# An attention kernel with a mixture-of-depths layer behind it: scatters that do not wait for each other, a reordered start, denominators in four column tiles, and sections of four attention steps with up to two pieces of the layers

## The chip, the cores and the metric

The kernel runs on one core of a Trainium2 chip. The metric is device time in microseconds (us), the median of the runs shown. A core has five engines with a queue each, which runs in order: TensorE (PE, its weight loads are PEld), VectorE (DVE), ScalarE (ACT), GpSimd (POOL) and SyncE (SP, which here only issues DMAs).

## The reference

```python
q_n, k_n = rmsnorm(q, g_q), rmsnorm(k, g_k)           # (8, 12, 448, 64), fp32
attn = softmax(q_n @ k_n.T / 8); x = attn @ v         # heads side by side: (8, 448, 768)
scores = x @ w_gate                                   # per batch: the 128 tokens of highest score
h = relu(x[top] @ w1); y = h @ w2                     # 768 -> 1024 -> 768
out = x; out[top] = x[top] + sigmoid(scores[top]) * y
```

Eight batches are independent of each other. The layers of a batch need its gate scores, and so all of its attention.

## The kernel before

**Units and groups.** Four heads of a batch are a group (24 groups, three per batch); a group's 448 keys are cut into 7 steps of 64, the *units* (168). `scores` of a unit (L252) fills two banks of `ps_sc` (four banks in all), ACT turns them into `p` by an Exp (L261), `values` (L278) accumulates `p` times v into the group's two banks `av`, and `add_probs` (L291, DVE) adds the `p` of a group's units up. PE works in tiles of 64x32 there, and a group of 32 recorded matmuls is two units.

**End of a group.** ACT and DVE copy `av` out as `xT` (L303, L305); `sum_keys` (L315, called D below) adds `sum` over the partitions into `den_ps`; `invert_sums` (T, L331, L333) transposes it and takes reciprocals; `to_tokens` runs twice (X, L345, L347): PE transposes `xT` into `x_ps` and DVE multiplies it into the tokens `x`. D, T, X and the transposes R of the gate's scores share one bank, the only buffer of `ps_aux`.

**End of a batch.** DVE computes the gate (L368) and spreads it, R and a copy give `score_rows`, DVE ranks the tokens (`count`, L401, four instructions) and prepares the weights (`annotate`, L415 to L426), POOL scatters the chosen rows to DRAM by four indirect DMAs (`select`, L433), SP loads them back (`load_selected`, `xe`), and `mixture` transposes them (E, L463) and runs the two layers as eight *pieces* M (four of L480 and four of L497). The last piece ends in L506 and one indirect DMA into the output.

**Preparation of a group.** SP loads `tok` (queries and keys by token), `qT`, `kT` and `v`; ACT squares `tok` (L167), DVE sums (L173, L174), POOL takes the power -1/2 (`rinv`, L177); for the queries the result goes to DRAM and comes back broadcast (`rows_out`, `rows_in`: `rows`, `bc`), and DVE scales `qT` (L211). For group 0, PE broadcasts instead (L223).

**Order.** The program's order is written out by hand. A *section* is: scores of two units, values of the two units before, then what `at(slot, ...)` has put there, and one piece of `mixture` if it has one left. There are 84 sections. All waits follow from the data and the buffers.

Of the kernel before, what the change touches and what calls it, by code (L numbers as in the profile page):

```python
# [26 lines left out]
def fast(  # L27
# [23 lines left out]

    nc = tc.nc
# [22 lines left out]
    p_pool = ctx.enter_context(tc.tile_pool(name="p", bufs=6))  # L75
# [50 lines left out]
    nc.vector.memset(neg_half, -0.5)  # L126

# [12 lines left out]
    def constants():  # L140


        nc.vector.memset(earlier, -1.2e-38)
# [13 lines left out]
    def load_weights():  # L157
        nc.sync.dma_start(out=wg, in_=_bcast_row(moe_w_gate, CP))
        nc.sync.dma_start(out=w1, in_=moe_w1.rearrange("(c p) f -> p c f", p=128))
        nc.sync.dma_start(out=w2, in_=moe_w2.rearrange("(c p) f -> p c f", p=128))  # L160
# [3 lines left out]
    def squares(n, i):  # L164
        t = toks.pop((n, i))
        sq = norm_pool.tile([128, 2, NI, D], F32, name="sq", bufs=1)
# [144 lines left out]
    def sum_keys(n):  # L311

        ps = ps_aux.tile([128, 512], F32, tag="aux", name="den_ps")
        for hh in range(2):
            nc.tensor.matmul(  # L315
                out=ps[32 * hh : 32 * (hh + 1), 0:S],
                lhsT=pick_pair,
                rhs=sums[n][:, hh],
                start=True,
                stop=True,  # L320
            )
        sums.pop(n)
        den = norm_pool.tile([64, NJ, CP], F32, name="den", bufs=1)
        nc.scalar.copy(out=den, in_=ps[:64, 0:S].rearrange("d (p j) -> d j p", j=NJ))
        dens[n] = den

    def invert_sums(n):
        den = dens.pop(n)
        ps = ps_aux.tile([128, NJ, 64], F32, tag="aux", name="denT_ps")
        for j in range(NJ):  # L330
            nc.tensor.transpose(out=ps[:CP, j, :], in_=den[:, j, :], identity=ident[:64, :64])  # L331
        rden = norm_pool.tile([CP, NJ, 2, 2], F32, name="rden")
        nc.vector.reciprocal(  # L333
            out=rden, in_=ps[:CP].rearrange("p j (h r) -> p j h r", r=32)[:, :, :, 0:2]
        )
        rdens[n] = rden
# [26 lines left out]
    def gate(b, js):  # L363
        if js[0] == 0:
            gates[b] = moe_pool.tile([CP, NJ], F32, name="gate", bufs=2)
        for j in js:
            prod = moe_pool.tile([CP, DM], F32, name="prod")
            nc.vector.scalar_tensor_tensor(  # L368
                out=prod,
                in0=xs[b][:, j, 0:DM],  # L370
                scalar=1.0,
                in1=wg,
                op0=OP.mult,
                op1=OP.mult,
                accum_out=gates[b][:, j : j + 1],
            )

    def spread(b):

        t = moe_pool.tile([CP, NJ, CP], F32, name="spread")  # L380
        nc.vector.tensor_copy(out=t, in_=gates[b][:, :, None].to_broadcast([CP, NJ, CP]))
        rowss[b] = t
# [45 lines left out]
    def select(b):  # L428

        x, rank = xs.pop(b), ranks.pop(b)  # L430
        t = dram_pool.tile([CAP, DX], F32, name="selected")
        for j in range(NJ):
            nc.gpsimd.indirect_dma_start(  # L433
# [6 lines left out]
            )  # L440
        slots_dram[b] = t
# [8 lines left out]
    def mixture(b):  # L450
# [23 lines left out]
        yield  # L474
        hT = moe_pool.tile([128, NFC, 128], F32, name="hT")
        for f0 in range(0, NFC, 2):
            ps = ps_moe.tile([128, 512], F32, tag="moe", name="moe_ps")
            for i in range(2):
                for dc in range(NDC):
# [6 lines left out]
                    )  # L486
            nc.scalar.activation(  # L487
                out=hT[:, f0 : f0 + 2, :n],
                in_=ps[:, :256].rearrange("p (i t) -> p i t", t=128)[:, :, :n],
# [644 lines left out]
```

## Time and profile before

| | us |
|---|---|
| median of 3 runs (lowest, highest) | 658.07 (656.10, 661.79) |
| the profiled execution, its own time | 659.13 |
| its span, first to last instruction | 657.4 |
| PE busy in the span | 546.7 (83%) |
| DVE busy | 359.4 (55%) |
| ACT busy | 276.8 (42%) |
| POOL busy | 186.4 (28%) |
| mean granted TensorE clock | 0.928 of full |

The page divides the span by engine and shows it in 40 slices. Further views show the instructions in order of time with what ended the idle time before them, the waits by who waited for whom, and the busy time in any stretch.

### The profile page before, as it was taken

Reading aid. Unit: us, or ns where it says so; the run is one execution under the profiler, and the core shown is the slowest. Engines: PE = TensorE matmul, PEld = TensorE weight load, DVE = VectorE, ACT = ScalarE, POOL = GpSimd, SP = SyncE. Lnnn points to the kernel's source line nnn. Section 1 sums busy time; section 2 is a strip of 40 time slices with the busy share of each in tenths; the row PEclk is TensorE's granted clock in tenths of the full one; section 3 lists DMA queues with packets and bytes.
Section 4 is the critical chain, followed back from the end, with each engine's and each line's share of the span. In section 5 each row is a group of like instructions: output and inputs, shape, how many; then the busy total and the mean of one; then the engine's idle time right before and its main releaser. Section 6 shows DMA issues by size and latency. Waiting matters only on the chain.

```text
span 657.4 us, 15932 instructions
## 1 busy us (share of the span) xinstructions
PE 546.7 (83%) x6920; PEld 282.4 (43%) x6920; DVE 359.4 (55%) x588; ACT 276.8 (42%) x497; POOL 186.4 (28%) x99
## 2 busy tenths in 40 slices
PE   1638988689997999499996999599998999797185
PEld 1213333246434554156433654256435643284182
DVE  1446879554873568454873558554876476335000
ACT  1335665544544545444543544444544544410000
POOL 2633442511154223412053232512055212100200
PEclk9959998879997999979996999989999999798589
DMA  7975556172706534272806534273706331102200
GB/s 247 397 266 169 171 197 225 41 245 104 251 22 197 195 109 169 67 236 86 253 20 205 187 91 167 68 230 112 252 27 220 113 114 35 40 1 84 72 1 28
DMA packets 46914, 93.99 MB, mean 143 GB/s; under 512 B 11510, under 2 KB 29686, under 8 KB 46836
## 3 DMA queue, kind: packets, MB, share of 16 engines
q1 hardware_dynamic: 43492, 86.58, 39.9%
q0 software_dynamic: 3200, 6.31, 2.9%
q8 instruction: 56, 0.92, 0.6%
q14 instruction: 22, 0.18, 0.1%
q10 hardware_dynamic: 144, 0.00, 0.0%
HBM read 75.39 MB, written 25.36 MB: 153 GB/s over the span
## 4 chain that ended last, share of the span: by engine, by line
PE 53%; issue 21%; DMA 10%; POOL 7%; DVE 5%; ACT 3%; POOLq 0%; SPq 0%; DVEq 0%; ACTq 0%
PE sc L252 16%; PE av L278 13%; PE moe_ps L480 10%; PE moe_ps L497 7%; POOL selected L433 4%; DMA selected<-x,rank 4%; DMA xe<-selected 4%; PE x_ps L345 3%; DMA tok<-in_tok_dram 2%; POOL rinv L177 2%; ACT p L261 2%; DVE ss L173 2%; PE den_ps L315 1%; PE denT_ps L331 1%; DVE sum L291 1%
## 5 line engine op out<-in xcount | busy, mean ns | idle before, releaser
L261 ACT ACTIVATE p<-sc,rinv 128x448 f32<-128x448 f32 x336 | 186.5, 634 | 156.8 <-PE sc L252 141.2
L177 POOL TENSOR_TENSOR rinv<-ss,neg_half 128x14 f32<-128x14 f32 x48 | 136.7, 2848 | 300.6 <-DVE ss L174 280.2
L252 PE MATMUL sc<-qT,kT 64*32 64x448 f32 x2688 | 162.8, 588 | 15.9 <-ACT p L261 11.3
L278 PE MATMUL av<-p,v 64*32 64x448 f32 x2688 | 154.1, 556 | 7.3 <-ACT xT L303 7.3
L291 DVE TENSOR_TENSOR sum<-sum,p 128x896 f32<-128x896 f32 x120 | 129.3, 1077 | 4.7
L480 PEld LDWEIGHTS moe_ps<-xeT,w 128*128 128x128 f32 x768 | 90.5, 196 | 14.9 <-ACT p L261 11.0
L480 PE MATMUL moe_ps<-xeT,w 128*128 128x128 f32 x768 | 95.4, 282 | 1.5 <-ACT hT L487 1.5
L278 PEld LDWEIGHTS av<-p,v 64*32 64x32 f32 x2688 | 54.1, 111 | 90.1 <-issue 73.1
L497 PE MATMUL moe_ps<-w,hT 128*128 128x384 f32 x256 | 91.1, 502 | 1.9 <-DVE xe L506 1.4
L252 PEld LDWEIGHTS sc<-qT,kT 64*32 64x32 f32 x2688 | 46.6, 111 | 83.9 <-issue 60.6
L173 DVE TENSOR_REDUCE ss<-sq 128x14 f32<-128x896 f32 x48 | 51.9, 1080 | 35.1 <-ACT sq L167 35.1
L433 POOL DMA_INDIRECT selected<-x,rank x32 | 38.7, 1210 | 95.0 <-DVE x L426 46.6
L497 PEld LDWEIGHTS moe_ps<-w,hT 128*128 128x128 f32 x256 | 47.1, 193 | 41.7 <-issue 10.3
L347 DVE TENSOR_TENSOR x<-x_ps,rden 112x512 f32<-112x512 f32 x48 | 33.1, 690 | 40.5 <-PE x_ps L345 39.7
L167 ACT ACTIVATE sq<-tok 128x896 f32<-128x896 f32 x48 | 46.2, 962 | 14.8 <-DMA tok<-in_tok_dram 10.2
L487 ACT ACTIVATE hT<-moe_ps 128x256 f32<-128x256 f32 x32 | 12.3, 383 | 88.4 <-PE moe_ps L480 88.4
L345 PE MATMUL x_ps<-ident,xT 128*112 128x128 f32 x192 | 30.5, 281 | 11.9 <-DVE x L347 11.5
L463 PE MATMUL moe_ps<-ident,xe 128*128 128x128 f32 x24 | 6.5, 401 | 40.7 <-DMA xe<-selected 40.7
L506 DVE SCALAR_TENSOR_TENSOR xe<-moe_ps,xe 128x384 f32<-128x384 f32 x16 | 9.9, 618 | 53.2 <-PE moe_ps L497 53.1
L211 DVE SCALAR_TENSOR_TENSOR qT<-qT,gg,bc 128x896 f32<-128x896 f32 x23 | 26.4, 1148 | 17.3 <-DMA bc<-rows 17.3
L345 PEld LDWEIGHTS x_ps<-ident,xT 128*112 128x112 f32 x192 | 20.3, 133 | 32.7 <-DVE x L347 14.0
L305 DVE COPY xT<-av 128x448 f32<-128x448 f32 x24 | 15.0, 624 | 31.0 <-PE av L278 31.0
(54 smaller groups left out, 242.5 us busy)
## 6 DMA issues: line engine op xcount, KB each, us to landing
tok<-in_tok_dram SPq DMA_DIRECT2D x48, 448.0 KB, 6.5
qT<-in_qT_dram SPq DMA_DIRECT2D x24, 448.0 KB, 5.8
kT<-in_kT_dram SPq DMA_DIRECT2D x24, 448.0 KB, 7.6
v<-in_vp_dram SPq DMA_DIRECT2D x24, 448.0 KB, 7.6
out_dram<-x SPq DMA_DIRECT2D x8, 1344.0 KB, 7.3
bc<-rows SPq DMA_DIRECT2D x46, 224.0 KB, 4.0
w<-in_moe_w_dram SPq DMA_DIRECT2D x2, 3072.0 KB, 20.6
xe<-selected SPq DMA_DIRECT2D x8, 385.0 KB, 3.2
```

The source lines that it names most:

```text
L167: nc.scalar.activation(out=sq, in_=t, func=AF.Square, scale=scale)
L173: nc.vector.tensor_reduce(out=ss, in_=sq, axis=AX.X, op=OP.add)
L177: nc.gpsimd.tensor_tensor(out=rinv.rearrange(flat), in0=ss.rearrange(flat), in1=neg_half.to_broadcast([128, 2 * NI]), op=OP.pow,)
L252: nc.tensor.matmul(out=scs[hh][o : o + 32, 0:S], lhsT=kTs[n][r, c, D * i + k0 : D * i + k0 + 32], rhs=qTs[n][r, c, :], start=True, stop=True,)
L261: nc.scalar.activation(out=p[:, hh], in_=scs[hh][:, 0:S], func=AF.Exp, scale=rinvs[n, 1][:, hh, i : i + 1],)
L278: nc.tensor.matmul(out=avs[n][c][o : o + 32, 0:S], lhsT=vs[n][r, hh, i, d0 : d0 + 32], rhs=probs[u][r, hh], start=(i == 0), stop=(i == NI ...
L291: nc.vector.tensor_tensor(out=sums[n], in0=probs[u - 1] if i == 1 else sums[n], in1=probs[u], op=OP.add)
L345: nc.tensor.transpose(out=ps[:CP, j, :], in_=t[:, j, :], identity=ident)
L347: nc.vector.tensor_tensor(out=xs[b][:, :, col : col + 128].rearrange("p j (h d) -> p j h d", d=D), in0=ps[:CP].rearrange("p j (h d) -> p j ...
L433: nc.gpsimd.indirect_dma_start(out=t[:, :], out_offset=bass.IndirectOffsetOnAxis(ap=rank[:, j : j + 1], axis=0), in_=x[:, j, :], in_offset ...
L480: nc.tensor.matmul(out=ps[:, 128 * i : 128 * i + n], lhsT=w1[:, dc, 128 * (f0 + i) : 128 * (f0 + i + 1)], rhs=xeT[:, dc, :n], start=(dc == 0),
L497: nc.tensor.matmul(out=ps[:n, : DM // 2], lhsT=hT[:, fc, :n], rhs=w2[:, fc, cols], start=(fc == 0), stop=(fc == NFC - 1),)
```

## The change

- `select`: the four scatters of a batch are declared independent, so that none waits for the one before to land.
- Start: both `tok` of groups 0 and 1 are squared first, `sq` gets a second buffer, group 1 is prepared ahead of the first scores, and all loads of group 1 stand ahead of the weights, which are loaded in 14 parts at slots 8 to 21. An Exp on one column stands ahead of the first square; `earlier` is set by POOL.
- `values_out`: both copies of `av` on ACT, contiguous (the order of the queries is changed on the host).
- `sum_keys`: four matmuls of 224 columns on four column tiles in place of two of 448; `invert_sums` transposes twice in place of four times.
- `gate`: per group (four instructions of 256 columns each) in place of per batch (four of 768).
- `mixture`: `hT` is filled in fours; the last batch's layers use the banks of `ps_sc`.
- Order: a section is two *halves* (two units each, the values always of the half before, then the half's slots), and then up to two pieces of `mixture`. D, T, X and R are a list of tasks; one of them may go ahead of the first piece and one behind each piece. The section with E holds one piece. There are 42 sections until the last scores, numbered q0 to q41 below.

```diff
-    p_pool = ctx.enter_context(tc.tile_pool(name="p", bufs=6))
+    p_pool = ctx.enter_context(tc.tile_pool(name="p", bufs=7))
...
+    load_tok(0, 1)
     load_q(0)
-    load_tok(0, 1)
     load_k(0)
-    load_v(0)
     load_tok(1, 0)
     load_tok(1, 1)
+    load_v(0)
     load_q(1)
+    load_k(1)
+    load_v(1)
...
+    warm = const.tile([128, 1], F32, name="warm")
+    nc.scalar.activation(out=warm, in_=neg_half, func=AF.Exp)
...
-            src = avs[n][c][:, 0:S].rearrange("d (p j) -> d j p", j=NJ)
-            if c == 0:
-                nc.scalar.copy(out=t, in_=src)
-            else:
-                nc.vector.tensor_copy(out=t, in_=src)
+            nc.scalar.copy(out=t.rearrange("d j p -> d (j p)"), in_=avs[n][c][:, 0:S])
...
+            for odd in range(2):
+                o = 64 * odd + 32 * hh
+                nc.tensor.matmul(
+                    out=ps[o : o + 32, 0 : S // 2],
+                    lhsT=pick_pair,
...
+        for jj in range(NJ // 2):
+            nc.tensor.transpose(out=ps[:CP, jj, :], in_=den[:, jj, :], identity=ident)
...
-    def gate(b, js):
+    def gate(n):
...
-        for j in js:
-            prod = moe_pool.tile([CP, DM], F32, name="prod")
+        cols = slice(GH * D * g, GH * D * (g + 1))
+        for j in range(NJ):
+            prod = moe_pool.tile([CP, GH * D], F32, name="prod")
...
+        writes = []
         for j in range(NJ):
-            nc.gpsimd.indirect_dma_start(
+            w = nc.gpsimd.indirect_dma_start(
...
+            for other in writes:
+                tc.declare_no_dep(w.ins, other.ins, reason="different rows")
+            writes.append(w)
...
+        def bank():
+            if b == B - 1:
+                return ps_sc.tile([128, 512], F32, name="sc")
+            return ps_moe.tile([128, 512], F32, tag="moe", name="moe_ps")
...
+    for part in range(NDC + NFC):
+        at(8 + part, load_w, part)
+    at(9, constants)
...
+    def finish(n, q):
+        b, g = divmod(n, NG)
+        task((q, 1), sum_keys, n)
+        task((q, 2) if HALVES > 1 else (q + 1, 0), invert_sums, n)
+        task((q + 1, 0) if HALVES > 1 else (q + 1, 1), to_tokens, n, 0)
+        task((q + 1, 1) if HALVES > 1 else (q + 2, 0), last_tokens, n)
...
+    def last_tokens(n):
+        to_tokens(n, 1)
+        b, g = divmod(n, NG)
+        q = now[0]
+        at(PER * (q + 1), gate, n)
+        if g < NG - 1:
+            return
+        at(PER * (q + 1), store_x, b)
+        at(PER * (q + 1) + 1, spread, b)
+        task((q + 1, 1), ranks_of, b)
+
+    def ranks_of(b):
+        score_rows(b)
+        s = PER * (now[0] + 1)
+        at(s, count, b, (0, 1))
+        at(s + 1, count, b, (2, 3))
+        at(s + 2, annotate, b)
+        at(s + 2, select, b)
+        at(s + 3, load_selected, b)
+        ready.append((b, (s + 3) // PER + 4 // HALVES - 1))
...
+        for half in range(HALVES):
+            k = 2 * (HALVES * q + half)
+            for u in (k, k + 1):
+                if u < units:
+                    scores(u)
+            run_values(k - 1, q)
+            for slot in (k, k + 1):
+                for fn in todo.pop(slot, ()):
+                    fn()
+        opening(q, 0)
+        for half in range(HALVES):
+            end = next(moe, None)
+            if end is None and ready and q >= ready[0][1]:
+                moe = mixture(ready.pop(0)[0])
+                end = next(moe)
+                done += 1
+            opening(q, half + 1)
+            if end and HALVES > 1:
+                break
+        q += 1
```

PE's order at the turn to the third batch's layers (`moe_ps<-ident,xe` and `xeT_ps` are E, `x_ps` X, `den_ps` D, `denT_ps` T, `row_ps` R; 16 matmuls of `sc` or `av` are two units). Before:

```order
L345 MATMUL x_ps<-ident,xT 112x128 x8
L252 MATMUL sc<-qT,kT 32x448 x16
L278 MATMUL av<-p,v 32x448 x16
L252 MATMUL sc<-qT,kT 32x448 x16
L278 MATMUL av<-p,v 32x448 x16
L315 MATMUL den_ps<-sum,pick_pair 32x448 x2
L463 MATMUL moe_ps<-ident,xe 128x128 x3
L463 MATMUL xeT_ps<-ident,xe 128x128 x3
L331 MATMUL denT_ps<-ident,den 112x64 x4
L252 MATMUL sc<-qT,kT 32x448 x16
L278 MATMUL av<-p,v 32x448 x16
```

Now (from the end of q19 to the end of q21):

```order
L345 MATMUL denT_ps<-ident,den 112x128 x2
L266 MATMUL sc<-qT,kT 32x448 x16
L292 MATMUL av<-p,v 32x448 x24
L266 MATMUL sc<-qT,kT 32x448 x16
L292 MATMUL av<-p,v 32x448 x16
L359 MATMUL x_ps<-ident,xT 112x128 x8
L266 MATMUL sc<-qT,kT 32x448 x16
L292 MATMUL av<-p,v 32x448 x16
L266 MATMUL sc<-qT,kT 32x448 x16
L292 MATMUL av<-p,v 32x448 x16
L488 MATMUL moe_ps<-ident,xe 128x128 x3
L488 MATMUL xeT_ps<-ident,xe 128x128 x3
```

E stands two sections of two units behind X before, and one section of four units behind it now; no piece M lies between them in either.

DVE's order in the section in which that batch is ranked (q20; `cmp` is `count`, `rank` to `x<-token_f` is `annotate`, `ss` the sums of squares, `qT` the scaling). Before, the same batch:

```order
L401 SCALAR_TENSOR_TENSOR cmp,higher<-score_rows,gate,earlier 112x448 x2
L506 SCALAR_TENSOR_TENSOR xe<-moe_ps,xe 128x384
L173 TENSOR_REDUCE ss<-sq 128x14
L174 TENSOR_SCALAR ss<-ss 128x14
L415 CAST rank<-higher 112x4
...
L426 TENSOR_SCALAR x<-token_f 112x4
L333 RECIPROCAL rden<-denT_ps 112x16
L291 TENSOR_TENSOR sum<-sum,p 128x896 x2
L347 TENSOR_TENSOR x<-x_ps,rden 112x4x128 x2
```

Now:

```order
L305 TENSOR_TENSOR sum<-p 128x896
L305 TENSOR_TENSOR sum<-sum,p 128x896
L187 TENSOR_REDUCE ss<-sq 128x14
L421 SCALAR_TENSOR_TENSOR cmp,higher<-score_rows,gate,earlier 112x448 x2
L225 SCALAR_TENSOR_TENSOR qT<-qT,gg,bc 128x896
L421 SCALAR_TENSOR_TENSOR cmp,higher<-score_rows,gate,earlier 112x448 x2
L305 TENSOR_TENSOR sum<-sum,p 128x896 x2
L187 TENSOR_REDUCE ss<-sq 128x14
L188 TENSOR_SCALAR ss<-ss 128x14
L435 CAST rank<-higher 112x4
...
L446 TENSOR_SCALAR x<-token_f 112x4
L361 TENSOR_TENSOR x<-x_ps,rden 112x4x128 x2
```

All that DVE does for a section of four units stands now ahead of the first product `x<-x_ps`, for which the second X of PE waits, since both use the one bank. Before, `annotate` came a section after `count`, and L506 of the layers stood between them.

SP's order at the start. Before:

```order
L91 DMA tok<-in_tok_dram 128x896
L91 DMA qT<-in_qT_dram 128x2x448
L91 DMA tok<-in_tok_dram 128x896
L91 DMA kT<-in_kT_dram 128x2x448
L91 DMA v<-in_vp_dram 128x896
L91 DMA tok<-in_tok_dram 128x896 x2
L91 DMA qT<-in_qT_dram 128x2x448
L158 DMA wg<-in_moe_w_gate_dram 112x768
L159 DMA w_143<-in_moe_w_dram 128x6x1024
L160 DMA w_144<-in_moe_w_dram 128x8x768
L91 DMA kT<-in_kT_dram 128x2x448
L91 DMA v<-in_vp_dram 128x896
```

Now:

```order
L92 DMA tok<-in_tok_dram 128x896 x2
L92 DMA qT<-in_qT_dram 128x2x448
L92 DMA kT<-in_kT_dram 128x2x448
L92 DMA tok<-in_tok_dram 128x896 x2
L92 DMA v<-in_vp_dram 128x896
L92 DMA qT<-in_qT_dram 128x2x448
L92 DMA kT<-in_kT_dram 128x2x448
L92 DMA v<-in_vp_dram 128x896
L204 DMA rows<-rinv 64x2x7 x2
L216 DMA bc<-rows 64x2x448 x2
L92 DMA tok<-in_tok_dram 128x896 x2
L92 DMA qT<-in_qT_dram 128x2x448
```

The weights (`w`, `wg`) are no longer ahead of group 1's keys and values; they come in parts behind the loads of groups 2 and 3. The `tok` of group 2 (shown last but one) stands behind `rows` and `bc` of group 1.

## Rows read from the trace of the kernel before

**Rows 1.** Busy time by stage (stretch, length, busy us by engine, PEclk, DMA):

```profile
50.50:135.00 84.50, 67.80 (x1121) 26.73 (x1108) 58.92 (x90) 50.35 (x88) 31.61 (x14) 0.94 0.50 163
135.00:575.00 440.00, 402.60 (x5214) 206.00 (x5214) 265.37 (x429) 205.30 (x373) 128.50 (x63) 0.95 0.44 141
575.00:657.40 82.40, 55.64 (x322) 40.73 (x322) 16.10 (x37) 5.82 (x14) 5.68 (x6) 0.86 0.11 37
```

**Rows 2.** Timeline of the start, SP, ACT and PE (start, length, instruction, [idle before]):

```profile
12.31 9.81 SPq L91 DMA_DIRECT2D kT<-in_kT_dram  x1
...
37.70 0.95 ACT L167 ACTIVATE sq<-tok 128x896 f32<-128x896 f32 x1 [10.24 <-DMA tok<-in_tok_dram]
...
50.50 2.14 PE L252 MATMUL sc<-qT,kT 64*32 64x448 f32 x32
```

**Rows 3.** Chain of waits, from the start, first `tok` (start, length, what):

```profile
4.04 3.48 DMA tok<-in_tok_dram
```

**Rows 4.** Timeline of PE, a section and the next one's start, at full clock:

```profile
297.32 1.73 PE L252 MATMUL sc<-qT,kT 64*32 64x448 f32 x32
...
300.49 0.95 PE L315 MATMUL den_ps<-sum,pick_pair 128*32 128x448 f32 x4
301.37 2.94 PE L480 MATMUL moe_ps<-xeT,w 128*128 128x128 f32 x24
304.24 0.43 PE L331 MATMUL denT_ps<-ident,den 64*112 64x64 f32 x4
304.61 1.74 PE L252 MATMUL sc<-qT,kT 64*32 64x448 f32 x32
```

**Rows 5.** PE's waits (who <- for whom: us in all, times, longest):

```profile
PE moe_ps L463 <- DMA xe<-selected: 40.7, 8, 14.1
...
PE x_ps L345 <- DVE x L347: 11.5, 10, 2.0
...
PE av L278 <- ACT xT L303: 7.3, 6, 1.4
...
PE row_ps L388 <- DVE spread L381: 4.6, 2, 2.4
...
PE moe_ps L480 <- ACT hT L487: 1.5, 3, 0.5
```

**Rows 6.** Chain of waits at one batch's turn:

```profile
328.48 2.88 POOL rinv L177
...
332.17 1.58 POOL selected L433
...
342.46 4.98 DMA selected<-x,rank
...
347.46 3.66 DMA xe<-selected
```

**Rows 7.** The scatters, line L433 (ns min/median/max; then landing):

```profile
L433 POOL DMA_INDIRECT selected<-x,rank x32: 940/943/2407, 117.4 to 615.6; - x32
...
DMA to landing us min/median/max: 2.5/2.8/5.0
```

**Rows 8.** DVE's instructions by line (count | busy us, mean ns | idle before):

```profile
L291 DVE TENSOR_TENSOR sum<-sum,p 128x896 f32<-128x896 f32 x120 | 129.3, 1077 | 4.7
L173 DVE TENSOR_REDUCE ss<-sq 128x14 f32<-128x896 f32 x48 | 51.9, 1080 | 35.1 <-ACT sq L167 35.1
L347 DVE TENSOR_TENSOR x<-x_ps,rden 112x512 f32<-112x512 f32 x48 | 33.1, 690 | 40.5 <-PE x_ps L345 39.7
L368 DVE SCALAR_TENSOR_TENSOR prod<-x,wg 112x768 f32<-112x768 f32 x32 | 30.6, 955 | 0.8
L211 DVE SCALAR_TENSOR_TENSOR qT<-qT,gg,bc 128x896 f32<-128x896 f32 x23 | 26.4, 1148 | 17.3 <-DMA bc<-rows 17.3
L401 DVE SCALAR_TENSOR_TENSOR cmp<-score_rows,gate,earlier 112x448 f32<-112x448 f32 x32 | 21.8, 682 | 0.9 <-ACT score_rows L392 0.3
```

**Rows 9.** Busy time in one stretch at half clock:

```profile
276.60:286.90 10.30, 6.98 (x66) 3.16 (x74) 4.14 (x6) 4.12 (x7) 0.00 (x0) 0.50 0.96 292
```

More of the change, by code (lines that the diff above doesn't have):

```diff
@@ L155, in constants, with load_w @@
         nc.vector.tensor_copy(out=token_f, in_=token_i)
[L157 to L160, printed above, removed]
+    def load_w(part):
+        if part == 0:
+            nc.sync.dma_start(out=wg, in_=_bcast_row(moe_w_gate, CP))
+        for w, src in ((w1, moe_w1), (w2, moe_w2)):
+            n = w.shape[1]
+            if part < n:
+                nc.sync.dma_start(
+                    out=w[:, part], in_=src.rearrange("(c p) f -> p c f", p=128)[:, part]
+                )
+            part -= n
+            if part < 0:
+                return
     def squares(n, i):
         t = toks.pop((n, i))
-        sq = norm_pool.tile([128, 2, NI, D], F32, name="sq", bufs=1)
+        sq = norm_pool.tile([128, 2, NI, D], F32, name="sq")
         nc.scalar.activation(out=sq, in_=t, func=AF.Square, scale=scale)
@@ L314, in sum_keys @@
         for hh in range(2):
[L315 to L321, printed above, removed]
+            for odd in range(2):
[3 more added lines that the diff above has]
+                    lhsT=pick_pair,
+                    rhs=sums[n][:, hh].rearrange("k (jj odd p) -> k odd jj p", odd=2, p=CP)[
+                        :, odd
+                    ],
+                    start=True,
+                    stop=True,
+                )
         sums.pop(n)
-        den = norm_pool.tile([64, NJ, CP], F32, name="den", bufs=1)
-        nc.scalar.copy(out=den, in_=ps[:64, 0:S].rearrange("d (p j) -> d j p", j=NJ))
+        den = norm_pool.tile([128, NJ // 2, CP], F32, name="den", bufs=1)
+        nc.scalar.copy(out=den.rearrange("d j p -> d (j p)"), in_=ps[:, 0 : S // 2])
         dens[n] = den
@@ L520, in mixture, with task, opening, prepare @@
                 )
-            yield
+            yield True
+    HALVES = 2
+    PER = 2 * HALVES
     units = n_groups * NI
-    todo = {}
+    todo, tasks = {}, []
     def at(slot, fn, *args):
         todo.setdefault(slot, []).append(lambda: fn(*args))
-    def prepare(n, slot, step):
+    def task(when, fn, *args):
+        tasks.append((when, lambda: fn(*args)))
+    def opening(q, place):
+        if tasks and tasks[0][0] <= (q, place):
+            tasks.pop(0)[1]()
+    def prepare(n, slot):
@@ L573, in fast @@
-    for i in range(2):
-        sum_squares(0, i, squares(0, i))
-        if i == 0:
-            scale_q_early(0)
-    constants()
-    load_weights()
-    moe, pending = iter(()), list(range(B))
-    k = 0
-    while 2 * k < units + 2 or todo or pending:
-        for u in (2 * k, 2 * k + 1):
-            if u < units:
-                scores(u)
-        late = 2 * k - 1 if (2 * k - 1) % NI == 0 else None
-        for u in (2 * k - 2, 2 * k - 1):
-            if 0 <= u < units and u != late:
-                values(u)
-                add_probs(u)
-                if u % NI == NI - 1:
-                    values_out(u // NI)
-        for fn in todo.pop(2 * k, ()):
-            fn()
-        if next(moe, moe) is moe and pending and k >= first_k[pending[0]]:
-            moe = mixture(pending.pop(0))
-            next(moe)
-        if late is not None and late < units:
-            values(late)
-            add_probs(late)
-        for fn in todo.pop(2 * k + 1, ()):
-            fn()
-        k += 1
+            prepare(n, s0 - 12)
@@ new lines, in run_values @@
+    def run_values(upto, q):
+        ended = False
+        while waiting and waiting[0] <= upto:
+            u = waiting[0]
+            if ended and u % NI == 0:
+                return
+            values(waiting.pop(0))
+            if u % NI == NI - 1:
+                values_out(u // NI)
+                finish(u // NI, q)
+                ended = True
+            add_probs(u)
+    sq = {}
+    sq[0, 0] = squares(0, 0)
+    sum_squares(0, 0, sq.pop((0, 0)))
+    sq[0, 1] = squares(0, 1)
@@ new lines, in fast @@
+    sum_squares(0, 1, sq.pop((0, 1)))
+    sq[1, 0] = squares(1, 0)
+    sq[1, 1] = squares(1, 1)
+    scale_q_early(0)
+    sum_squares(1, 0, sq.pop((1, 0)))
+    rows_out(1)
+    sum_squares(1, 1, sq.pop((1, 1)))
+    rows_in(1)
+    waiting = list(range(units))
+    moe, ready, done, q = iter(()), [], 0, 0
+    while done < B:
+        now[0] = q
+        for half in range(HALVES):
[18 more added lines that the diff above has]
+        q += 1
```

98 lines of the change are left out of this document (41 added, 57 removed).

## The prediction

> **What bounds the kernel now.** I read the busy time by stage first [rows 1]. The stages are cut at scores that can be named: from the scores of units 8 and 9 at 50.5 [rows 2] to those of units 40 and 41 at 135.0 there is attention alone; then come layers beside attention for 440 us, until the last group's last values; the tail takes 82.4. The reader is to see that PE has 402.6 of the 440 us busy while DVE has 265.4 and ACT 205.3, and that the granted clock is 0.95 there: this stage is PE's work, with holes. In the attention stage PE is at 80% and DVE at 70%. The second view is the start [rows 2, 3]: SP needs 9.8 us to issue one load behind the 6 MB of weights, and ACT waits 10.2 us for `tok` of group 2. The third is PE's list of waits [rows 5]: `xe` is by far the largest, 26.6 us in seven turns and 14.1 in the last one. The fourth, the chain of waits at one turn [rows 6], says why: from the first scatter at 332.17 to `xe` at 351.12 it is 18.95 us, of which the four scatters, each waiting for the last to land, are 15.3. A hole also costs the clock: in 276.6 to 286.9 the granted clock is 0.50, the lower level, and PE is busy for 6.98 us [rows 9], which is 3.5 lost. The 440 us at 0.95 hold some 44 us at the lower level in six turns; at 6.98/10.3 busy that is 30 us of work, 15 lost.
>
> The sum is made against the profiled execution, 659.1; the median is 658.1, 1 less.
>
> **Start (to the scores of unit 8): -13.5, between -20 and -6.** Group 1 no longer stands behind the weights, but `tok` of group 2 is now behind `rows` and `bc` of group 1 in SP's queue, and these wait for POOL. By hand: the scaling of group 0 ends at about 18.2 (0.6 later than now, since the extra Exp ahead of the first square waits for a DVE constant that comes behind a load); a sum of squares 1.3 [rows 8]; `rinv` 2.6 to 2.9 [rows 6]; `rows` out, small, 1.3 to issue and about 2.8 to land (the landing of a scatter [rows 7] as the nearest small DMA); `bc` 1.3 to issue; `tok` 3.5 [rows 3]. That is 30.5 to 31, against 37.7 now. Square and two Exps later unit 6 begins, and unit 8 at 37 in place of 50.5. Low end: `tok` as soon as SP is free; high end: as late as now, with the rest earlier.
>
> **Attention alone, units 8 to 39 (sections q2 to q9): 84.5 to 78, -6.5, between -14 and +2.** Two units of scores and values take PE 3.17 [rows 4]; DVE needs an addition of 1.08 per unit, and per group two sums of squares (1.3 each), the scaling 1.15 and two products of 0.69 [rows 8]. The gate comes to four instructions of 256 columns; between 0.68 for 448 and 0.96 for 768 columns [rows 8] I take 0.57 each with the reading of the sum, 2.3 per group. By PE's work and, where X, T or R wait for it, DVE's queue ahead, the eight sections take 7.2, 8.4, 10.9, 6.5, 9.3, 7.7, 13.5 and 10.7, 74.2 in all, and I add 4 for the clock. Three of them are set by DVE, not by PE.
>
> **Layers beside attention (q10 to q41): 440 to 419, -21, between -45 and +12.**
> - D takes 0.88 and T 0.37 [rows 4]; half the columns and half the transposes save about 0.55 in each of 18 groups, **-10**. Nothing hides it, PE is the bound. PE changes half as often between attention and other work; no row has the price of one change alone, so I take 0, and 30 of 0.3 (a tenth of a piece's 2.87 [rows 4]) for the low end.
> - The values of a new group wait for `xT` 7.3 us in all [rows 5]; ACT's copies now lie under the scores that stand ahead of these values: **-4** in this stage. The copy that leaves DVE (0.6 per group) is worth nothing by itself.
> - X's wait for DVE, **+8**. It is 11.5 in ten waits now [rows 5]. In the section that ranks a batch the whole of DVE's work stands ahead of the first product. q20: 0.7 left over, four additions 4.3, two sums 2.5, four `count` of 0.73 2.9, scaling 1.15, `annotate` about 1.3: 12.8. PE comes to X at 6.8, its second X waits 6.1. By the same addition the waits are 2.4 (q13), 1.0, 6.1, 1.1, 0.7, 2.3 (q29) and 1.8: 15.4 in place of 7.
> - `xe`, **-10.6**. Without mutual waits the chain is 1.6, then three of 0.94 and 0.15 to the issue of the last [rows 7], 2.8 to land and 3.4 for `xe`: 10 us in place of 15 to 19. It starts later, though: in q20 `annotate` ends at 12.8, POOL has a `rinv` of 2.9 ahead [rows 6], `xe` is there at 24.5, and E is reached at 20.2. I get waits of 6.4 (batch 1), 4.5 (2), 0, 0 and 1.3 (5), 12.2 in all, where 22.8 stand now. Batches 3 and 4 have a section with pieces in between, which covers the chain.
> - Clock: three holes in place of six, **-5** of the 15 lost.
>
> **Tail: 82.4 to 75.5, -7, between -15 and 0.** The last `xe` waits 14.1 [rows 5]; now one piece of the first layer and four of the second, 13.4 us, stand between R and E, and the chain behind R (copy 0.9, `count` 2.9, `annotate` 1.4, scatters and `xe` 10.3) is 16: a wait of 3, **-11**. The spread that R waits 2.4 for is there at once, and the last layers, on four banks, don't wait for `hT` [rows 5]: **-5**. Against it E of batch 6 moves into the tail with its transposes and a wait of 7.5, since only two units of values cover its chain: **+9**.
>
> At nothing I cost `earlier` on POOL (idle until the first scatters) and the seventh `p`; a `p` too few would show as ACT waiting for DVE. The weights in 14 parts are covered by attention: they are due at E of the first batch, some 40 us after the last part.
>
> Sum: -13.5 - 6.5 - 21 - 7 = **-48**, 611 for the profiled execution, **610** for the median.
>
> One rule of the skill speaks against the scatters. Of 32 issues the median is 0.943 us, while DVE is busy 60% of the stage, and the longest is 2.407 [rows 7]: most are not held up. The Trainium skill, page "SBUF — State Buffer", section "Who interferes with whom", says that a DMA issued from GpSimd is starved while a Vector instruction in a two-port mode holds the port pair that both share. By that rule four issues in a row, no longer spread over 12 us, can all stand behind DVE; the trace bears it out for the few long ones at most.
>
> **Rivals.**
> 1. *X and `xe` hardly wait* (chance 0.15). If DVE gets through a section sooner than my addition says (its instructions overlap by some 0.05 each, and it may start on the additions during the pieces), the 15.4 and 12.2 shrink to a third and the clock keeps its level: -18 and -10 more, **580**. For: X's longest wait now is 2.0 [rows 5]. Against: the ranking section takes 12.1 us of DVE by rows.
> 2. *The start gains nothing* (0.12). The weights in parts lie between the loads of groups 2 to 5, and SP issues in order; if these fill the DMA engines as they do now, squares wait there and not here: +14, **624**. For: one load took 9.8 us to issue [rows 2]. Against: the parts come at two per half.
> 3. *The scatters are held up* (0.08). At 2.4 in place of 0.94 each, the chain is 4.4 longer in six turns that wait, +26, and +5 for the clock: **641**. For: 2.407 occurs [rows 7]. Against: the median.
> 4. *DVE becomes what PE waits for, in the sections with layers too* (0.07), the slow end. DVE works its queue in order, and a section's products for X stand behind all its additions, sums, gates and scalings: 9.3 us on average by the rows above, when X or T asks at 6.3 to 9. If every one of some 24 sections with pieces waits 2.5 us more than I have counted, it is 60 us more, **671**, slower than now by 2%. It decides from 2 us per such section, 48 in all. Against: a piece covers 2.87 [rows 4], and two cover the average.
>
> **How the numbers follow.** My forecast, 590 to 632 by itself, has 0.58, and the rivals 0.42. The time predicted is that of the forecast, 610. The range of 8 in 10 goes from 580, rival 1, to 642, rival 3, and leaves out rival 4 and what lies below rival 1. A measurement of this kernel tells about 1%, 6.6 us, from no change: faster by more than that means below 651.5. Forecast and rivals 1, 2 and most of 3 lie there; with what I may have overlooked: faster 0.88, same 0.06, slower 0.06.
>
> **What would show it.** Right: scores of unit 8 near 37; X waiting for DVE in the ranking sections, 15 us in all; `xe` waits of batches 3 and 4 gone, those of 1, 2 and 6 still 4 to 8; four scatters within 5 us of POOL; a last wait under 5. Wrong: ACT waiting for `tok` in groups 3 to 5; PE's `x_ps` waits above 40 us in all; scatters of 2 us each; a granted clock no higher than 0.93 on the whole.

## The result, and the profile after

The changed kernel takes **599.95 us** (median of four runs, 598.43 to 603.11), the kernel before 657.95 in the same comparison: a ratio of 0.9118, 95% interval 0.9063 to 0.9173. The forecast was 610, so the time is 10 us below it. The profiled execution has a span of 596.7 us, with the granted clock at 0.957 on the whole where it was 0.928. In experiments 2 and 3 one of four runs was slow (1730 and 614 us), which is in the median given there and not in the ratio.

Busy time by stage of the kernel after, cut at the scores of units 8 and 40 and at the last group's last values (stretch, length, then for PE, PEld, DVE, ACT and POOL the busy us and the instructions; granted clock, DMA share, GB/s). It answers to [rows 1]:

```profile
0.00:41.06 41.06, 19.39 (x281) 9.06 (x289) 16.51 (x30) 15.66 (x24) 17.02 (x12) 0.88 0.58 202
41.06:125.18 84.12, 66.95 (x1122) 26.01 (x1107) 62.22 (x115) 50.82 (x92) 37.33 (x20) 0.90 0.74 252
125.18:528.00 402.82, 380.43 (x5288) 210.81 (x5284) 261.80 (x513) 205.37 (x377) 133.93 (x62) 0.99 0.46 151
528.00:596.70 68.70, 49.42 (x290) 37.88 (x290) 13.07 (x44) 6.26 (x13) 8.80 (x9) 0.90 0.17 55
```

Cut the same way, the kernel before has 50.5, 84.5, 445.3 and 77.1 us (its last group's values end at 580.3; [rows 1] were cut 5.3 us ahead of that, at 575.0). So the start gives 9.4 us, the tail 8.4, the layers beside attention 42.5, and the stage with attention alone gives 0.4. In the layers' stage the clock went to 0.99, and PE is busy for 380 of 403 us.

PE's waits after (who <- for whom: us in all, times, longest), which answer to [rows 5]:

```profile
PE x_ps L359 <- DVE x L361: 12.8, 8, 5.2
PE moe_ps L488 <- DMA xe<-selected: 10.6, 4, 8.5
PE x_ps L359 <- DVE rden L347: 10.5, 4, 4.3
...
PE denT_ps L345 <- ACT den L338: 6.0, 4, 2.4
```

`xe` has gone from 40.7 to 10.6 us, 8.5 of which are the one wait of batch 6. The waits for `xT` no longer appear, and the one for the spread is 0.2. X now waits longer than before, 25.0 us in all in place of 11.8, and 10.5 of it for `rden`, the reciprocal that belongs to T; before, that was one wait of 0.3.

The turn to the third batch's layers, POOL and SP by time (start, length, instruction, [idle before]):

```profile
263.45 2.58 POOL L191 TENSOR_TENSOR rinv<-ss,neg_half 128x14 f32<-128x14 f32 x1 [4.21 <-DVE rank L435]
266.20 1.00 POOL L454 DMA_INDIRECT selected<-x,rank  x1 [0.17 <-issue]
267.51 1.23 POOL L454 DMA_INDIRECT selected<-x,rank  x1 [0.30 <-issue]
269.04 1.15 POOL L454 DMA_INDIRECT selected<-x,rank  x1 [0.30 <-issue]
270.50 1.10 POOL L454 DMA_INDIRECT selected<-x,rank  x1 [0.30 <-issue]
273.28 0.33 SPq L472 DMA_DIRECT2D xe<-selected  x1
```

The four scatters follow each other at 0.30 us, `xe` is loaded at 273.28 and PE begins E at 276.6: 10.4 us from the first scatter, where [rows 6] have 18.95.

### The profile page after: what moved, and what is told of

It is laid out like the page before. It is cut to its first block, busy times and chain, and to the rows that moved or that the text cites. A ratio compares the mean times of both kernels' runs of the same rounds, so it can differ in the third digit from the quotient of the medians.

```text
span 596.7 us, 16194 instructions
## 1 busy us (share of the span) xinstructions
PE 516.2 (87%) x6968; PEld 283.8 (48%) x6968; DVE 353.6 (59%) x699; ACT 278.1 (47%) x506; POOL 197.1 (33%) x100
## 5 line engine op out<-in xcount | busy, mean ns | idle before, releaser
L191 POOL TENSOR_TENSOR rinv<-ss,neg_half 128x14 f32<-128x14 f32 x48 | 143.5, 2990 | 242.6 <-DVE ss L188 173.4
L266 PEld LDWEIGHTS sc<-qT,kT 64*32 64x32 f32 x2688 | 51.0, 110 | 82.8 <-issue 53.3
L511 PE MATMUL moe_ps<-xeT,w 128*128 128x128 f32 x672 | 81.5, 278 | 0.3 <-ACT hT L520 0.3
L511 PEld LDWEIGHTS moe_ps<-xeT,w 128*128 128x128 f32 x672 | 78.1, 194 | 5.2 <-issue 4.7
L530 PE MATMUL moe_ps<-w,hT 128*128 128x384 f32 x224 | 77.6, 491 | 1.4 <-DVE xe L539 0.7
L361 DVE TENSOR_TENSOR x<-x_ps,rden 112x512 f32<-112x512 f32 x48 | 33.1, 690 | 62.5 <-PE x_ps L359 60.4
L454 POOL DMA_INDIRECT selected<-x,rank x32 | 37.2, 1162 | 67.8 <-DVE x L446 50.1
L530 PEld LDWEIGHTS moe_ps<-w,hT 128*128 128x128 f32 x224 | 40.5, 190 | 28.6 <-issue 2.1
L385 DVE SCALAR_TENSOR_TENSOR prod<-x,wg 112x256 f32<-112x256 f32 x96 | 40.6, 423 | 2.5
L548 POOL DMA_INDIRECT out_dram<-xe,row x8 | 12.0, 1495 | 80.1 <-DVE rden L347 48.8
L520 ACT ACTIVATE hT<-moe_ps 128x512 f32<-128x512 f32 x14 | 8.4, 597 | 59.5 <-PE moe_ps L511 59.5
L305 DVE TENSOR_TENSOR sum<-p 128x896 f32<-128x896 f32 x24 | 25.7, 1072 | 2.5 <-ACT p L275 2.5
## 6 DMA issues: line engine op xcount, KB each, us to landing
w<-in_moe_w_dram SPq DMA_DIRECT2D x6, 512.0 KB, 10.1
```

What stands on the lines that cost most here:

```text
L191: nc.gpsimd.tensor_tensor(out=rinv.rearrange(flat), in0=ss.rearrange(flat), in1=neg_half.to_broadcast([128, 2 * NI]), op=OP.pow,)
L266: nc.tensor.matmul(out=scs[hh][o : o + 32, 0:S], lhsT=kTs[n][r, c, D * i + k0 : D * i + k0 + 32], rhs=qTs[n][r, c, :], start=True, stop=True,)
L305: nc.vector.tensor_tensor(out=sums[n], in0=probs[u - 1] if i == 1 else sums[n], in1=probs[u], op=OP.add)
L385: nc.vector.scalar_tensor_tensor(out=prod, in0=xs[b][:, j, cols], scalar=1.0, in1=wg[:, cols], op0=OP.mult, op1=OP.mult, accum_out=gates[b ...
L454: w = nc.gpsimd.indirect_dma_start(out=t[:, :], out_offset=bass.IndirectOffsetOnAxis(ap=rank[:, j : j + 1], axis=0), in_=x[:, j, :], in_of ...
L511: nc.tensor.matmul(out=ps[:, 128 * i : 128 * i + n], lhsT=w1[:, dc, 128 * (f0 + i) : 128 * (f0 + i + 1)], rhs=xeT[:, dc, :n], start=(dc == 0),
```

## The experiments

Each ratio is to the kernel before, timed on the same chip. Where two ratios are compared, the interval of the difference is the root of the squares of their half widths, times 658 us.

**1. The scatters alone.** The kernel before, and in `select` only:

```diff
-            nc.gpsimd.indirect_dma_start(
+            w = nc.gpsimd.indirect_dma_start(
...
+            for other in writes:
+                tc.declare_no_dep(w.ins, other.ins, reason="different rows")
+            writes.append(w)
```

> The kernel before, with the four scatters of a batch declared independent and nothing else changed. Theory: the waits for xe (26.6 us in seven turns, 14.1 in the last) come from the scatters waiting for each other; the chain from the first scatter to xe falls from 15-19 us to about 10, so the seven waits all but vanish and the last is 6 to 8: 34 us less by the waits and 5 to 10 by the clock, 612 to 622. Rival: another wait (x_ps, hT, spread) takes their place, or the scatters, four in a row, take 2.4 us each: 640 or more.

622.94 us, ratio 0.9486 (0.9424 to 0.9547): 34 us less, 0.9 us above the range that the theory gave. The wait went as the theory had it, by 32 us, and is left in one turn, the last:

```profile
PE moe_ps L467 <- DMA xe<-selected: 8.8, 1, 8.8
```

The time at the lower clock falls from 94 us to 47, and PE is busy for 533.5 us in place of 546.7. Its other waits grew (X's from 11.8 to 15.9), which takes part of it back. More than half of the whole gain is in this one edit.

**2. All but the scatters.** The changed kernel, without the declaration:

```diff
-                tc.declare_no_dep(w.ins, other.ins, reason="different rows")
+                pass
```

> The changed kernel, with the scatters waiting for each other again. Theory: the chain is 6 to 7 us longer and stands bare in the turns of batches 1, 2, 6 and 7, whose xe was there just in time; in 3 and 4 a section covers it: 25 us and some clock, 622 to 632, the xe waits 35 in all. Rival: the longer sections cover the chain by themselves: below 608.

643.04 us, ratio 0.9762 (0.9676 to 0.9849): 42 us (7 either way) more than the changed kernel. The turn to the third batch's layers on POOL, and PE's waits:

```profile
285.05 1.00 POOL L454 DMA_INDIRECT selected<-x,rank  x1 [0.17 <-issue]
287.96 1.09 POOL L454 DMA_INDIRECT selected<-x,rank  x1 [1.91 <-DMA selected<-x,rank]
291.08 0.94 POOL L454 DMA_INDIRECT selected<-x,rank  x1 [2.04 <-DMA selected<-x,rank]
293.89 0.94 POOL L454 DMA_INDIRECT selected<-x,rank  x1 [1.86 <-DMA selected<-x,rank]
```

```profile
PE moe_ps L488 <- DMA xe<-selected: 41.8, 6, 10.1
```

41.8 us is what the kernel before had (40.7): in all, the longer sections gain nothing on the chain. They cover it in batches 3 and 4, and the other turns wait longer. Of the 42 us, 31 are this wait; beside the other 11 stand 109 us at the lower level in place of 51, and 14.0 us more of busy time on PE. The theory's bare turns (batches 1, 2, 6 and 7) came; batches 0 and 5, which it did not name, wait 4.4 and 6.3 us as well, so its sum (25 and some clock) was too small.

**3. Sections of one half.**

```diff
-    HALVES = 2
+    HALVES = 1
```

> The changed kernel with sections of one half (two units) and one piece each, the tasks in the places that the program has for that. Theory: the two-half section is worth a little, since PE is the bound either way: 605 to 620, with the attention stage still at 80 to 86 because DVE sets it. Rival: the x_ps waits on DVE (23 us) are made by the long sections, whose additions all stand ahead of the products; then they fall to 12 or less, and the time is 590 to 598.

605.18 us, ratio 0.9207 (0.9130 to 0.9283): 6 us more than the changed kernel, with 6 either way, so no difference that these runs can tell. PE's waits at X for DVE and for `rden` fall from 23.3 to 11.1 us, as the rival said, but E's second bank then waits 19.2 (`xeT_ps` for DVE's `row`), and the stage with attention alone stays at 83.5. The time and the stage lie in the theory's range, X's waits in the rival's: the long section makes waits at X, but it is not what makes that stage long.

**4. Less work for DVE.**

```diff
-            nc.vector.tensor_tensor(
+            if i == 1 or i == NI - 1:
+                nc.vector.tensor_tensor(
```

> The changed kernel without 96 of its 144 additions of p (the sums over the keys leave four units of seven out): DVE has 104 us less to do. Theory: DVE's queue makes the holes at X and T and the length of the attention stage; the 23 us of x_ps waits fall below 6, the stage of units 8 to 39 goes from 84 to 70-75, and the whole to 560-580. Rival: PE and the order of its own work set the stage; the time stays within 6 us of 600.

This kernel leaves four of seven units out of the sums. 590.08 us, ratio 0.8985 (0.8930 to 0.9039). DVE is busy for 255.1 us in place of 353.6, and the time falls by 9 (5 either way), 8 of it in the layers' stage. The stage with attention alone takes 83.85 us where it was 84.12: the theory falls. X's waits fall from 23.3 to 12.7, not below 6, and those for `rden` in this stage from 7.9 to 6.6 only: the one near 110 from 4.3 to 1.8, while the one near 69 rises from 3.5 to 4.7. DVE around the latter, without the additions:

```profile
61.65 1.09 DVE L187 TENSOR_REDUCE ss<-sq 128x14 f32<-128x896 f32 x1 [2.06 <-ACT sq L181]
...
66.19 1.15 DVE L225 SCALAR_TENSOR_TENSOR qT<-qT,gg,bc 128x896 f32<-128x896 f32 x1 [3.25 <-DMA bc<-rows]
67.26 1.08 DVE L187 TENSOR_REDUCE ss<-sq 128x14 f32<-128x896 f32 x1
68.37 0.18 DVE L188 TENSOR_SCALAR ss<-ss 128x14 f32<-128x14 f32 x1
68.45 0.25 DVE L348 RECIPROCAL rden<-denT_ps 112x16 f32<-112x16 f32 x1
```

The reciprocal that PE waits for stands behind the scaling, and the scaling now stands idle for `bc`. In the changed kernel two additions fill that time, and the reciprocal ends no later: 28.3 us behind the scores of unit 8, where it is 29.5 here. What delays it is its place in the queue, not the queue's load.

**5. `tok` of group 2 first.**

```diff
+    load_tok(2, 0)
+    load_tok(2, 1)
     rows_out(1)
     sum_squares(1, 1, sq.pop((1, 1)))
```

> The changed kernel with the two loads of tok of group 2 issued ahead of rows and bc of group 1 in SP's queue. Theory: ACT's wait of 7.2 us for tok in the start is made by that queue alone; the scores of unit 8 come at 33 to 36 in place of 41.1 and the time is 592 to 596. Rival: tok would not land earlier beside the other loads, or the next thing (rinv, bc of group 2) is late by as much: 598 to 601.

596.80 us, ratio 0.9051 (0.9015 to 0.9087): 4.4 us less (4.3 either way), just outside the 592 to 596 that were expected. The place was right: unit 8 is reached at 33.2 in place of 41.1, and the granted clock from 18 to 33 is 1.00. But the next stage is 3.8 us longer: the wait of X for `rden` that begins near 59 is 6.0 us in place of 3.5. The scaling ahead of that reciprocal, which needs `bc`, now has DVE idle for 2.3 us until a DMA lands.

**6. Denominators as before.** Two matmuls of 448 columns on two column tiles in `sum_keys`, four transposes of 64 in `invert_sums`:

```diff
-            for odd in range(2):
-                o = 64 * odd + 32 * hh
...
+                out=ps[32 * hh : 32 * (hh + 1), 0:S],
...
-        for jj in range(NJ // 2):
+        for j in range(NJ):
```

> The changed kernel with the denominators as before: two matmuls of 448 columns, and four transposes (the copy between them stays contiguous). Theory: PE has 0.55 us more in each of 24 groups and nothing hides it: 13 us more, 610 to 615. Rival: the four tiles bring nothing, since the work lies under waits or runs one after another in any case: 598 to 603.

620.45 us, ratio 0.9403 (0.9363 to 0.9444): 18.8 us more (4.5 either way), above the expected 13. PE's lines of the denominators (count | busy us, mean ns | idle before), first of this kernel, then of the changed one:

```profile
L325 PE MATMUL den_ps<-sum,pick_pair 128*32 128x448 f32 x96 | 24.7, 596 | 5.0 <-ACT xeT L489 3.2 <-ACT score_rows L408 1.0 <-DVE x L357 0.8
L341 PE MATMUL denT_ps<-ident,den 64*112 64x64 f32 x96 | 10.6, 232 | 5.6 <-ACT den L334 5.6
```

```profile
L327 PE MATMUL den_ps<-sum,pick_pair 128*32 128x224 f32 x192 | 14.4, 374 | 5.2 <-ACT xeT L493 3.5 <-ACT score_rows L412 1.0 <-DVE x L361 0.8
L345 PE MATMUL denT_ps<-ident,den 128*112 128x128 f32 x48 | 10.3, 298 | 6.0 <-ACT den L338 6.0
```

These lines differ by 10.6 us of PE's busy time, nearly all of it in D; the transposes cost the same in twos as in fours. The other 8 are not in these lines: `xe` is waited for 6.3 us longer, 62.7 us lie at the lower clock in place of 51.1, and PE's busy time differs by 17.9 us in all (534.1 and 516.2).

**7. The task ahead of the first piece moved up.**

```diff
+            if half == HALVES - 1:
+                opening(q, 0)
+                for u in late:
+                    add_probs(u)
             for slot in (k, k + 1):
                 for fn in todo.pop(slot, ()):
                     fn()
-        opening(q, 0)
```

> The changed kernel with one move: in each section the task that stands ahead of the first piece is written ahead of the second half's additions and slots (sums of squares, scaling, gate, count) in place of behind them, so that its reciprocal or product stands ahead of them on DVE. Theory: the holes at X are made by DVE's order, not by its load; the x_ps waits fall from 23 us to below 12, the stage of units 8 to 39 from 84 to 76-80, the time to 585-594. Rival: DVE then stands waiting for PE at that task and the second half's work comes too late for the next section; the holes move to sc or to D: 600 or more.

607.91 us, ratio 0.9218 (0.9184 to 0.9253): 6.6 us more (4.3 either way). X's waits did fall, from 23.3 to about 11, but the rival won. The stage with attention alone takes 90.8 us, where the theory had 76 to 80 and the changed kernel 84.1; the tail is 3.8 longer. What DVE had to do for the ranks came later, and `xe` is waited for 24.8 us in place of 10.6.

```profile
PE moe_ps L488 <- DMA xe<-selected: 24.8, 4, 12.3
PE x_ps L359 <- DVE x L361: 10.6, 6, 4.3
```

Near 70 the reciprocal is early, and the product of X now stands where the reciprocal stood: a hole of 4.3 us again. D, T and X follow each other on PE there, so moving one of them up moved the hole to the next.

**8. Two pieces kept for the hole in the tail.**

```diff
+            if (q, half) == (39, 1):
+                opening(q, 2)
+                break
             end = next(moe, None)
```

> The changed kernel with two pieces of batch 5 moved two sections later (section q39 and q40 hold one piece, q41 two). Theory: the wait of 8.5 us for xe of batch 6 has nothing to cover it, and the two pieces do: the wait falls to 2-3 and the stretch at the lower clock behind it goes, 590 to 596. Rival: the pieces only trade places with the wait of the next task: 598 to 602.

596.66 us, ratio 0.9039 (0.9002 to 0.9075): 5.2 us less (4.3 either way), a little short of what was expected. The wait for `xe` of batch 6 falls from 8.5 to 3.9, the tail from 68.7 to 64.7, the time at the lower clock in it from 13.5 to 8.6.

**9. Weights in half the stream** (on top of 5).

```diff
-        at(8 + part, load_w, part)
+        at(8 + 2 * part, load_w, part)
```

> The kernel with tok of group 2 loaded first, and its 14 weight parts at every second slot (8 to 34) in place of every slot. Theory: the hole of 6.0 us at X near 59-65 is made by DMA: rows land 5.2 us late behind the weights, so bc, the scaling and the reciprocal behind it on DVE are late; with half the weights per time that hole falls below 2.5, the stage of units 8 to 39 goes from 88 to 81-84, the time to 589-593. Rival: it is DVE's own queue, and the hole stays: 595 to 598.

595.21 us, ratio 0.9029 (0.8994 to 0.9065), not to be told from experiment 5. The hole is 3.5, as in the changed kernel: less than the 6.0 of experiment 5, but not below 2.5. `rows` are still waited for (19.9 us by SP in 35 to 100, 18.6 in experiment 5), though half as many weights pass. The scaling no longer waits for a DMA, so what is left of the hole is made by DVE's order, as the rival had it.

**10. Experiments 5, 8 and 9 together.**

> tok of group 2 first, the weights at every second slot, and the two pieces of batch 5 kept for q41, together. Theory: they act at three different places and add up: 584 to 589. Rival: what is won early is lost again at the next wait or at the lower clock: 592 or more.

588.59 us, ratio 0.8930 (0.8890 to 0.8971): 12 us less than the changed kernel, where experiments 8 and 9 give 5 and 6 by themselves: within the noise they add up.

**11. The ranks one slot earlier** (on top of 10).

```diff
-        at(s + 2, annotate, b)
-        at(s + 2, select, b)
-        at(s + 3, load_selected, b)
+        at(s + 1, annotate, b)
+        at(s + 1, select, b)
+        at(s + 2, load_selected, b)
```

> The same three edits, and annotate and the four scatters of a batch one slot earlier (ahead of the second half's additions, sums and scaling, and ahead of the rinv that stood before them on POOL), the load of xe with them. Theory: xe comes 3 to 5 us sooner, the waits of batches 2 and 6 (2 and 4 us) vanish, 3 to 7 us less than the three edits alone. Rival: xe is not what PE stands for there, since the additions and X come later by as much: within 2 us of the three edits alone.

583.94 us, ratio 0.8847 (0.8811 to 0.8884): 5.5 us less than 10 (3.6 either way). The tail has all of it (59.6 us in place of 65.1). PE waits for `xe` for 0.2 us, and in one more turn 1.7 at E, which the trace puts down to DVE.

**12. The tasks apart** (on top of 11). In the sections without pieces, `between` may take one task at each of four places: behind a half's scores and behind its values.

```diff
+    def between():
+        if tasks and tasks[0][2] <= place[0]:
+            tasks.pop(0)[1]()
+        place[0] += 1
...
+            if q < ALONE:
+                between()
             run_values(k - 1, q)
...
+            if q < ALONE:
+                between()
```

> The four edits, and in the sections without pieces (q0 to q9) the tasks of a group no longer stand side by side at the section's end: each stands alone between a half's scores and values or behind its values (D one place behind the group's end, T three, the products five and six). Theory: the attention stage is long because D, T and X follow each other with nothing of PE's between them, so that ACT's copy and DVE's reciprocal behind a full queue are waited for in full; the waits of T for den and X for rden there (2.4, 3.5 and 4.5 us) fall below 3 in all, with them the 17 us at the lower clock; the stage of units 8 to 39 goes from 86 to 71-77, the time to 569-576. Rival: DVE and ACT together, with squares, sums and scaling due at the same time, set the stage, and the holes come back at another place: stage 82 or more, time 579 or more.

577.08 us, ratio 0.8782 (0.8745 to 0.8820): 4 us less than 11 (3.5 either way), and the best of all, though 1 us above the range of the theory. The same four stages, cut at its own scores:

```profile
0.00:32.77 32.77, 16.55 (x281) 8.94 (x289) 15.09 (x29) 15.60 (x24) 15.41 (x12) 1.00 0.67 236
32.77:103.94 71.17, 62.41 (x1117) 22.78 (x1109) 56.66 (x96) 49.07 (x91) 30.42 (x15) 1.00 0.79 278
103.94:514.40 410.46, 384.21 (x5298) 209.96 (x5282) 269.18 (x533) 205.83 (x381) 141.50 (x68) 0.97 0.47 153
514.40:573.90 59.50, 47.34 (x290) 36.34 (x290) 13.06 (x44) 6.16 (x13) 6.66 (x7) 0.97 0.19 64
```

PE's waits in the stage with attention alone, first in the changed kernel (X for `rden`, T for ACT's copy), then here:

```profile
PE x_ps L359 <- DVE rden L347: 7.9, 2, 4.3
PE denT_ps L345 <- ACT den L338: 3.4, 2, 2.4
```

```profile
PE sc L266 <- issue: 5.3, 2, 2.8
PE sc L266 <- ACT p L275: 1.1, 1, 1.1
```

The stage takes 71.2 us in place of the 86.0 of experiment 11, at a granted clock of 1.00; the holes at T and at `rden` are gone from it, and two shorter ones ahead of scores are new. (Some 2 us of E lay before its end in 11 and lie behind it here; D, T, X and R are as many in both.) The theory is shown for this stage. Not all of it stays: the profiled span is 8.2 us shorter, not 15, for the first batch's layers begin at 131.6 in place of 116.9, and in that stretch X waits 4.8 for `rden` and 10 us pass at the lower clock.

## Why the prediction was right, and where it was wrong

**Start: right, 4 us too hopeful.** Forecast 37 for unit 8, measured 41.1. The kernel after, SP, ACT and PE by time; it answers to [rows 2]:

```profile
21.84 1.34 SPq L204 DMA_DIRECT2D rows<-rinv  x2
24.81 1.25 SPq L216 DMA_DIRECT2D bc<-rows  x2
26.16 1.01 SPq L92 DMA_DIRECT2D tok<-in_tok_dram  x2
31.56 0.95 ACT L181 ACTIVATE sq<-tok 128x896 f32<-128x896 f32 x1 [7.20 <-DMA tok<-in_tok_dram]
33.08 2.26 PE L266 MATMUL sc<-qT,kT 64*32 64x448 f32 x16 [5.50 <-ACT p L275]
```

`tok` stands behind `rows` and `bc` as worked out, and the square begins at 31.56 where 30.5 to 31 was forecast. Unit 6 begins at 33.1, and from there to unit 8 it takes 8.0 us, where the forecast left about 4. Part of that is the clock: from 30.2, inside the hole of 5.5 us, to 40.4 it is 0.50, and the scores of units 6 and 7 run at the lower level. In experiment 5, at 1.00, the same stretch still takes 6.2, with a hole of 2.5 in it; here one of 1.8 lies in it. (The terms of that sum, from 18.2 to the square, add up to 31.0 to 31.3 rather than 30.5 to 31.)

**Attention alone: this step failed.** The forecast had the stage at 78 us, three of its sections set by DVE's queue; it took 84.1. The addition without the clock was short by 9.9 us in all, 3.6 of them in q5 (q2 to q9 take 8.6, 9.6, 13.0, 10.1, 10.1, 8.3, 13.5, 10.9). And it priced DVE's work, which experiment 4 takes away without shortening the stage. DVE and PE in the changed kernel around one hole:

```profile
63.47 1.08 DVE L187 TENSOR_REDUCE ss<-sq 128x14 f32<-128x896 f32 x1 [2.06 <-ACT sq L181]
64.59 0.17 DVE L188 TENSOR_SCALAR ss<-ss 128x14 f32<-128x14 f32 x1
64.68 2.21 DVE L305 TENSOR_TENSOR sum<-sum,p 128x896 f32<-128x896 f32 x2
66.81 1.14 DVE L225 SCALAR_TENSOR_TENSOR qT<-qT,gg,bc 128x896 f32<-128x896 f32 x1
67.87 1.08 DVE L187 TENSOR_REDUCE ss<-sq 128x14 f32<-128x896 f32 x1
68.98 0.17 DVE L188 TENSOR_SCALAR ss<-ss 128x14 f32<-128x14 f32 x1
69.06 0.25 DVE L347 RECIPROCAL rden<-denT_ps 112x16 f32<-112x16 f32 x1
...
65.42 0.43 PE L345 MATMUL denT_ps<-ident,den 128*112 128x128 f32 x2
69.37 1.10 PE L359 MATMUL x_ps<-ident,xT 128*112 128x128 f32 x4 [3.52 <-DVE rden L347]
```

PE finished T at 65.9 and could start X only at 69.4. The queue ahead of `rden` begins with a square that ACT delivers late and holds a scaling that needs `bc`; T and X stand side by side on PE, with no piece between them in this stage, so the delay is bare. Each of the stage's three holes of over 2 us (3.5, 2.4 and 4.3) has a stretch at the lower clock in or right behind it, 17.1 us in all, which can cost up to 8.5, where I had added 4. Experiment 12 puts PE's own work between D, T and X, and these holes and the lower clock go.

**Layers: the mechanisms right, three terms mis-sized.** By the same cut the stage gave 42.5 us where 21 were forecast.
- `xe` was put at -10.6, with the last wait from 14.1 to 3, against 7.5 for batch 6: 14 us of waits, and 5 of clock. The waits fell by 30 (40.7 to 10.6), the time by 34 to 42 in experiments 1 and 2. The chain itself came out to the tenth: in q20 `xe` is there 24.5 us after the section's start, as forecast (to E it takes 10.4 us; its terms add up to 10.8 and were put at 10); but PE came to E at 23.0, not at 20.2, so 1.5 stood bare, not 4.5. In batch 1 it was 0.4, not 6.4. In q20 PE arrived later than my sections had it. The clock was put at 5 us; the stretches at the lower level cost more, for with 58 us more of them PE is busy 14.0 us longer in experiment 2.
- The column tiles and the transposes in twos were put at 0.55 a group, which is 13 in all 24; undoing them costs 18.8. D saves 0.43 a group in that experiment and T nothing; the rest is waits for `xe` and the clock.
- X's wait for DVE was forecast at 15.4 in this stage, 6.1 the longest; it is 12.3 (9.7 for the products and 2.6 for `rden`), 5.2 the longest. The longest stands in q20, where it was put.
- `xT` is no longer waited for, as forecast.

The single effects don't add up: the scatters are worth 34 us by themselves and 42 on top of the rest, the tiles 19, the start 9. With 42 that is 70 where 58 are measured. A late PE hides a late `xe`, so part of one edit's gain can be another's. The copies of `av`, the gate per group and `hT` in fours were not run by themselves, and what each is worth stays open.

**Tail: -8.4 where -7 was forecast,** by a cut that lay 5.3 us earlier, and the wait of batch 6 that was put at 7.5 is 8.5. The last wait is 0.7, not 3. Two slips of arithmetic are in that 3: five pieces of 2.87 [rows 4] are 14.4 us, not 13.4, and the chain's terms add up to 15.5, not 16, which leaves 1.1.

**The total owes something to luck.** By stage the change missed the forecast by +4 us (start), +6 (attention alone), -21.5 (layers) and -1 (tail), and the first two made up for part of the third. Of the signs of being right, the `xe` waits of batches 3 and 4, the last wait and X's waits came about as named; the `xe` waits of batches 1 and 2 (0.4 and 1.5), unit 8 and the scatters (5.4 us from the first to the end of the last in the turn above) did not. None of the signs of being wrong came.

**The rivals.** Of the first (X and `xe` hardly wait), the half about `xe` came true. The second did not: ACT waits for no `tok` behind group 2's, though `rows` were waited for while the weights passed. The fourth did not: it needed 48 us of X's waits beside the layers, and there are 12.3. The third neither; line L454 answers to [rows 7]:

```profile
L454 POOL DMA_INDIRECT selected<-x,rank x32: 936/960/2426, 111.8 to 560.5; - x32
```

Half of the 32 take no longer than 0.96 us, and in the turn shown above, with DVE at work beside them, four in a row take 1.0 to 1.23. Five take 1.57 to 2.43, and each of the five runs beside an addition `sum` of DVE, as here:

```profile
114.49 2.38 POOL L454 DMA_INDIRECT selected<-x,rank  x1 [0.30 <-issue]
114.98 1.08 DVE L305 TENSOR_TENSOR sum<-sum,p 128x896 f32<-128x896 f32 x1
```

In the 14 traces of this case 73 scatters take over 1.5 us, 71 of them beside such an addition; of 375 shorter ones 62 are. So scatters are held up, and nearly always beside an addition, but few are, and by 0.6 to 1.5 us each: the 32 take 37.2 us, where they took 38.7 one by one in the kernel before. The rule of the Trainium skill, page "SBUF — State Buffer", section "Who interferes with whom", is that a DMA issued from GpSimd is starved behind Vector instructions of certain modes. In which mode these additions run no run here shows, so whether the five are cases of it stays open; the 27 others take at most 1.23 us, with DVE busy for 59% of the span.

## What to carry to other kernels

A chain of small transfers that wait for each other's landing can cost more than its bare waits: cut it where the writes cannot meet; here part of the clock came back with it. Where several short tasks each go PE, another engine, PE, put PE's own work between them; here, moving one of them up in another engine's queue only moved the hole. Before calling an engine the bound of a stage, take a large part of its work away and see whether the stage moves.

## What was not expected of the hardware

- The clock and the holes. In the start the level falls inside a hole of 5.5 us and stays low for 10.2; with a hole of 2.5 near the same time (experiment 5) it stays at 1.00, while one of 2.4 us in the attention stage goes with 3.4 us at the lower level. In all, 94 us lie at the lower level before, 51 after, 27 in experiment 12.
- The 3.5 KB of `rows` are waited for 5.2 us by SP while weights pass (SP's wait in 44 to 70), where the median landing is 2.3 us. SP issues in order, so all loads stand behind that wait, and near 61 the DMA engines are idle. That the weights make `rows` late is not shown: with half of them per time (experiment 9) the longest such wait is 7.2 us.
- A matmul on a column tile of 224 columns takes 374 ns in the mean, one of 448 columns 596: half the columns cost 0.63 of the time, and D's 24 groups together 14.4 us in place of 24.7.
